# Loading and converting the weights of a fused FFT and MLP kernel: one queue in the order of use, one piece per chunk of x, and products that nobody reads

## The chip, the cores and the metric

The kernel runs on one core of a Trainium2 chip. The metric is the device time of one execution in microseconds (us). Engines are called by the names of the profile: PE is TensorE (PEld its weight loads), DVE is VectorE, ACT is ScalarE, POOL is GpSimd, SP is SyncE. A kernel counts as faster or slower if its fast runs differ from those of the kernel before by over 2%.

## The reference

```python
def _attn_ref(x):                       # x: (8, 3008, 256) float32
    X = np.fft.fft(x, axis=1)
    X = np.fft.fft(X, axis=2)
    return X.real.astype(np.float32)

def _moe_ref(x, w_in, w_out):           # x: (24064, 256), w_in: (256, 2048), w_out: (2048, 256), both float64
    h = x @ w_in
    relu6 = np.clip(h + 3.0, 0.0, 6.0)
    g = h * relu6 / 6.0
    return (g @ w_out).astype(np.float32)
```

The kernel takes the eight batches as four pairs. Along the sequence (3008 = 47 · 64) it does the transform in two stages: a first one of length 47 on folded input, and a second one of length 64. The transform along the 256 columns is multiplied into w_in once ("folding of w_in"). The MLP runs in steps: a step takes two blocks of 128 hidden features, makes products u and v, gates them (hardswish), combines the gated blocks and accumulates them against w_out, of which seven mixtures (G) stand ready.

## The kernel before

The weights arrive as float64; the kernel makes every piece (128 x 512 numbers) into float32, mostly by integer operations, before it is multiplied. There are 16 pieces, taken in pairs: pieces 0, 1, 2, 3, 6, 7, 8, 9 are of w_in, the others of w_out. `narrow_a` unpacks a piece on DVE (four instructions; ACT makes the exponent meanwhile), `narrow_b` adds the sign on DVE and multiplies, on DVE or POOL; `use_pair` folds two w_in pieces with the column transform on PE, or mixes two w_out pieces to G on POOL and ACT.

```python
    def load_w(j):                      # the piece's load, through SP's queue
        st = wpool.tile([P, 2 * WB], I32, tag="st", bufs=5, name="st")
        ...
            nc.sync.dma_start(out=o, in_=moe_w_in[i * P:(i + 1) * P, n * WB:(n + 1) * WB])

    def narrow_a(j):
        ...
        ts = nc.vector.tensor_scalar
        ts(ex[:], hi, 20, 0x7FF, op0=AL.logical_shift_right, op1=AL.bitwise_and)
        ...                                                     # three instructions on ACT
        ts(top[:], hi, 0xFFFFF, 0x100000, op0=AL.bitwise_and, op1=AL.bitwise_or)
        ts(low[:], lo, 8, 0xFFFFFF, op0=AL.logical_shift_right, op1=AL.bitwise_and)
        nc.vector.scalar_tensor_tensor(frac, low[:], 2.0 ** -24, top[:], op0=AL.mult, op1=AL.add)

    def narrow_b(j):
        nc.vector.scalar_tensor_tensor(ex[:], hi, -2 ** 31, ex[:], ...)
        eng = nc.vector if j < 6 else nc.gpsimd
        eng.tensor_tensor(o, frac, ex[:].bitcast(F32), op=AL.mult)

    # MLP, one step's gates: DVE makes u and v into t (with ACT), then
        gate(a[:, 0, :, 0:ns], t[:, 0, :, 0:ns], u[:, :, 0:ns])          # gate u, DVE
        for i in (slice(0, 2),) if nm == KC else (0, 1):
            gate(a[:, 1, i, 0:nm, ::-1], t[:, 1, i, 0:nm], v[:, i, 0:nm]) # gate v, DVE
    # combine(): three additions of the gated blocks on POOL, the same step

    # first pair, stage one: eight chunks of x
    for c in range(NXC):
        fold(first, c, 0, nc.gpsimd)
        fold(first, c, 1, nc.vector)
        if c + 3 < NXC:
            load_x(first, c + 3)       # a direct load and a gather of the partner rows
        if c in (2, 5):
            narrow_pair((c + 1) // 3)
        ...
        if c in (2, 5):
            use_pair((c + 1) // 3)
    # pieces 8 to 15 are converted and used in pairs at MLP steps 0, 1, 3 and 5 (8, 9 are loaded in stage one, the others a pair ahead)
```

## Time and profile before

| | before |
|---|---|
| time, median of four runs | 2080.24 us |
| last product of stage one ends | 84.1 us |
| first MLP accumulation starts | 130.80 us |
| eighth MLP accumulation starts | 189.55 us |
| from there to the end | PE full at full clock |

These are events of PE in the timeline. Their differences split the start into three stretches (stage one, the transition, the first eight steps), and whatever an edit wins must show in one of them. The third stretch runs from the first accumulation to the eighth; here are the two in PE's timeline. The columns are start, length (both in us), engine, line, operation, out<-in, the partitions and columns, and the number of instructions:

```profile
130.80 1.46 PE L320 MATMUL acc<-a,G 128*128 128x256 f32 x6
...
189.55 1.46 PE L320 MATMUL acc<-a,G 128*128 128x256 f32 x6
```

```profile
138.08 1.27 POOL L409 TENSOR_TENSOR st<-top,ex 128x512 f32<-128x512 f32 x1 [11.10 <-DVE ex L406]
```

Here a one-source instruction of the unpacking takes 0.42 us and the two-source one 0.69 us. The bracket says under which condition: before its product POOL had stood still for 11.10 us, and the whole unpacking (133.83 to 135.65 us) lies in that time.

### The profile page before, as it was taken

How to read it: one execution, taken by the hardware profiler on the slowest of the kernel's cores; microseconds unless marked ns; L12 is line 12 of the kernel's file. 1: busy time of each engine (PE TensorE's matmuls, PEld its weight loads, DVE VectorE, ACT ScalarE, POOL GpSimd, SP SyncE). 2: the span in 40 equal slices, each digit the busy share in tenths (PEclk: the TensorE clock that was granted, in tenths of full speed). 3: DMA queues.
4: the chain of work that ended last, by engine and by line, in shares of the span. 5: the costliest groups of instructions: out<-in, count | busy, mean ns of one | idle time of the engine just before them, and what ended most of it. 6: DMA issues, size and time to landing. Idle time of an engine off the chain costs nothing.

```text
span 2078.6 us, 28133 instructions
## 1 busy us (share of the span) xinstructions
PE 1974.6 (95%) x9136; PEld 1692.0 (81%) x9136; DVE 1456.9 (70%) x2714; ACT 706.1 (34%) x1205; POOL 1496.1 (72%) x1662
## 2 busy tenths in 40 slices
PE   4468999999999999999999999999999999999997
PEld 1246888888888888888888888888888888888886
DVE  5366676776777677677677677677777777777775
ACT  2344333333333333333333333333333323333332
POOL 6248777877667887788667778778766766766765
PEclk7688999999999999999999999999999999999999
DMA  6420211221110122212111112211110011011000
GB/s 188 142 86 15 57 49 34 50 47 33 29 31 23 44 51 51 51 33 54 29 21 34 43 34 48 51 43 47 31 36 11 17 23 21 18 24 21 16 16 18
DMA packets 158161, 86.81 MB, mean 42 GB/s; under 512 B 132512, under 2 KB 145056, under 8 KB 158016
## 3 DMA queue, kind: packets, MB, share of 16 engines
q1 hardware_dynamic: 129856, 60.28, 12.7%
q0 software_dynamic: 28160, 24.73, 4.5%
q8 instruction: 74, 1.21, 0.3%
q14 instruction: 71, 0.58, 0.1%
HBM read 47.65 MB, written 37.22 MB: 41 GB/s over the span
## 4 chain that ended last, share of the span: by engine, by line
PE 91%; DVE 4%; DMA 2%; ACT 1%; issue 1%; POOL 1%; SPq 0%; DVEq 0%; POOLq 0%; ACTq 0%
PE acc L320 53%; PE v L266 16%; PE u L266 15%; PE ps L193 2%; PE ps L221 2%; PE wps L446 1%; PE ps L237 1%; DVE a L298 1%; DMA st<-in_moe_w_in_dram 1%; ACT t L295 1%; DVE u L279 0%; DVE ex L406 0%; DVE s L271 0%; PE wns L451 0%; DMA g<-zd 0%
## 5 line engine op out<-in xcount | busy, mean ns | idle before, releaser
L310 POOL TENSOR_TENSOR c<-a 128x512 f32<-128x512 f32 (+1 forms) x384 | 479.2, 1248 | 406.7 <-DVE a L298 258.7
L320 PE MATMUL acc<-c,G 128*128 128x256 f32 (+1 forms) x3072 | 714.1, 375 | 0.0
L320 PEld LDWEIGHTS acc<-c,G 128*128 128x128 f32 x3072 | 579.3, 191 | 73.8 <-POOL c L310 0.2
L295 ACT ACTIVATE t<-u,half 128x512 f32<-128x512 f32 (+2 forms) x416 | 272.3, 655 | 1074.8 <-DVE u L279 1063.2
L271 DVE SCALAR_TENSOR_TENSOR s<-qn,WN,u 128x256 f32<-128x256 f32 x768 | 334.4, 477 | 392.2 <-PE u L266 391.9
L320 PE MATMUL acc<-a,G 128*128 128x256 f32 (+1 forms) x2304 | 553.6, 377 | 0.0
L320 PEld LDWEIGHTS acc<-a,G 128*128 128x128 f32 x2304 | 436.8, 191 | 57.3
L266 PE MATMUL v<-q,W 128*128 128x256 f32 x1536 | 398.8, 382 | 17.9 <-DVE a L298 17.9
L266 PE MATMUL u<-q,W 128*128 128x256 f32 x1536 | 394.5, 379 | 0.0
L266 PEld LDWEIGHTS v<-q,W 128*128 128x128 f32 x1536 | 291.3, 191 | 64.3 <-issue 21.9
L266 PEld LDWEIGHTS u<-q,W 128*128 128x128 f32 x1536 | 287.4, 190 | 65.3 <-issue 20.9
L298 DVE SCALAR_TENSOR_TENSOR a<-t,u 128x512 f32<-128x512 f32 (+2 forms) x416 | 265.9, 646 | 105.3 <-ACT t L295 101.0
L310 POOL TENSOR_TENSOR c<-a,c 128x256 f32<-128x256 f32 (+1 forms) x384 | 275.0, 716 | 30.1
L310 POOL TENSOR_TENSOR c<-c,a 128x256 f32<-128x256 f32 (+1 forms) x384 | 275.0, 716 | 30.1
L279 DVE TENSOR_TENSOR u<-s,v 128x512 f32<-128x512 f32 (+1 forms) x384 | 263.0, 685 | 42.6 <-PE v L266 2.5
L295 ACT ACTIVATE t<-v,half 128x512 f32<-128x512 f32 (+1 forms) x384 | 257.0, 669 | 5.3 <-DVE v L285 4.4
L285 DVE TENSOR_TENSOR v<-v,s 128x512 f32<-128x512 f32 (+1 forms) x384 | 257.7, 671 | 1.1
L298 DVE SCALAR_TENSOR_TENSOR a<-t,v 128x512 f32<-128x512 f32 (+1 forms) x416 | 255.1, 619 | 0.1
L310 POOL TENSOR_TENSOR r<-w,e 128x256 f32<-128x256 f32 (+1 forms) x96 | 92.3, 982 | 3.8
L193 PE MATMUL ps<-y,F 94*96 94x512 f32 x120 | 67.0, 656 | 26.2 <-DVE y L159 20.1
L326 ACT ACTIVATE e<-acc 128x512 f32<-128x512 f32 (+1 forms) x192 | 87.0, 543 | 2.9 <-PE acc L320 2.8
L346 DVE STREAM_TRANSPOSE o<-r 128x256 f32<-128x256 f32 (+1 forms) x192 | 72.4, 415 | 6.5 <-POOL r L310 6.4
(70 smaller groups left out, 826.7 us busy)
## 6 DMA issues: line engine op xcount, KB each, us to landing
out_dram<-o SPq DMA_DIRECT2D x736, 32.0 KB, 1.6
zd<-z SPq DMA_DIRECT2D x32, 384.0 KB, 3.0
g<-zd SPq DMA_DIRECT2D x48, 256.0 KB, 4.2
xt<-in_x_dram POOLq DMA_DIRECT2D x28, 376.0 KB, 3.9
st<-in_moe_w_in_dram SPq DMA_DIRECT2D x8, 512.0 KB, 4.4
st<-in_moe_w_out_dram SPq DMA_DIRECT2D x8, 512.0 KB, 5.7
T<-in_c_stage_dram SPq DMA_DIRECT2D x12, 128.0 KB, 7.2
xt<-in_x_dram POOLq DMA_DIRECT2D x4, 282.0 KB, 3.4
```

Source lines behind the costliest of these rows:

```text
L193: nc.tensor.matmul(ps[0:PZ], F[0:PR, 0:PZ], y[:, 2 * i:2 * i + 2, :], start=True, stop=True)
L221: nc.tensor.matmul(ps[:, blk, 2 * u:2 * u + 2], g[:, kk, blk * P:(blk + 1) * P], T[:, :, gr, blk, kk], start=True, stop=True)
L266: nc.tensor.matmul(ps[:, i], W1[:, blk, f * P:(f + 1) * P], q[:, blk, of:of + KC], start=True, stop=True)
L271: nc.vector.scalar_tensor_tensor(s[:, i].rearrange("p k n -> p (k n)"), qn[:, of * N2:(of + KC) * N2], WN[:, f:f + 1], u[:, i].rearrange(" ...
L279: nc.vector.tensor_tensor(u[:, :, 0:ns], s[:, :, 0:ns], v[:, :, 0:ns], op=AL.add)
L285: nc.vector.tensor_tensor(v[:, :, 0:nm], v[:, :, 0:nm], s[:, :, 0:nm], op=AL.subtract)
L295: nc.scalar.activation(t, h, AF.Relu, bias=half[:], scale=scale)
L298: nc.vector.scalar_tensor_tensor(dst, t, 1.0, h, op0=AL.min, op1=AL.mult)
L310: nc.gpsimd.tensor_tensor(out, in0, in1, op=AL.add)
L320: nc.tensor.matmul(ch.acc[i // 2][:, i % 2, 0:ch.n], G[:, i, fc, :], mv, start=(fc == 0 and i % 2 == 0), stop=(fc == NF - 1), skip_group_c ...
L326: nc.scalar.mul(ch.e[:, k:i + 1, 0:ch.n], ch.acc[i // 2][:, 0:i + 1 - k, 0:ch.n], 1.0 / WS)
L346: nc.vector.transpose(o[:, 0:n // DH, h], ch.r[:, m, h, 0:n].rearrange("p (j i) -> p j i", i=DH))
```

## The change

The intent is to have every weight piece land and be converted just before its use. Loads of x and of weights share POOL's queue, in the order of use; in stage one, one piece is converted per chunk of x; the last four pieces are converted in halves behind the first MLP steps; PE multiplies zeros ("awake" products, which nobody reads) where it would wait, so that its clock stays up. P6 changes its sign so that ACT's negations fall away, and the first two mixings of w_out move from POOL to DVE. The diff, cut to its core:

```diff
-        st = wpool.tile([P, 2 * WB], I32, tag="st", bufs=5, name="st")
+        st = wpool.tile([P, 2 * WB], I32, tag="st", bufs=6, name="st")
-            nc.sync.dma_start(out=o, in_=moe_w_in[...])
+            nc.gpsimd.dma_start(out=o, in_=moe_w_in[...])          # w_out alike
-        ex = wpool.tile([P, WB], I32, tag="ex", bufs=2, name="ex") # top alike
+        ex = wpool.tile([P, WB], I32, tag="ex", name="ex")
-        eng = nc.vector if j < 6 else nc.gpsimd
+        eng = nc.vector if j < 12 else nc.gpsimd
-        tt = nc.gpsimd.tensor_tensor    # in the mixing of w_out
+        tt = (nc.vector if j < 2 else nc.gpsimd).tensor_tensor
-        nc.scalar.mul(g[5], g[5], -1.0)
...
+    load_t(0)
+    load_forward(first, 0)
+    load_w(0)
+    load_w(1)
+    load_partners(first, 0)
+    for c in (1, 2):
         load_x(first, c)
+        load_w(c + 1)
...
+    def keep_awake(n):
+        ps = ps_h.tile([P, 2 * TB], F32, tag="uv", name="awake")
+        for i in range(n):
+            nc.tensor.matmul(ps[:], ones[:], Z[:], start=True, stop=True)
...
         fold(first, c, 0, nc.gpsimd)
-        fold(first, c, 1, nc.vector)
         if c + 3 < NXC:
             load_x(first, c + 3)
-        if c in (2, 5):
-            narrow_pair((c + 1) // 3)
+        load_w(c + 4)
+        fold(first, c, 1, nc.vector)
+        if c > 1:
+            narrow_b(c)
+        if c > 0:
+            narrow_a(c + 1)
...
+        if c % 2 and c > 1:
+            use_pair(c // 2)
+        else:
+            keep_awake(3)
...                                     # pieces 8 to 11 are converted ahead of the MLP
-                put(t, narrow_pair, 4 + i)
-                put(t, use_pair, 4 + i)
+            for t, f, j in ((0, narrow_a, 12), (1, narrow_b, 12), (1, narrow_a, 13), (2, narrow_b, 13), (2, use_pair, 6),
+                            (3, narrow_a, 14), (4, narrow_b, 14), (4, narrow_a, 15), (5, narrow_b, 15), (5, use_pair, 7)):
+                after.setdefault(t, []).append((f, (j,)))
...
         mlp2(*chunk(s))
+        for f, a in after.get(s, ()):
+            f(*a)
```

More of the change, by code (lines that the diff above doesn't have):

```diff
@@ L47 @@
 NK1 = (N1 + 1) // 2
-PROD = ("P1", "P2", "-P4", "P5", "P7", "P6", "P3")
+PROD = ("P1", "P2", "-P4", "P5", "P7", "-P6", "P3")
 @with_exitstack
@@ L116, in __init__ @@
             self.p = p
-            self.x, self.y, self.z = {}, {}, {}
+            self.x, self.xr, self.y, self.z = {}, {}, {}, {}
             self.zd = None
@@ L131, in load_x, with load_forward @@
     def load_x(pr, c):
-        xt, xr = x_tile(pr, 2 * c), x_tile(pr, 2 * c + 1)
+        load_forward(pr, c)
+        load_partners(pr, c)
+    def load_forward(pr, c):
+        xt = x_tile(pr, 2 * c)
         rows = x_pn[pr.p * PR:(pr.p + 1) * PR]
@@ L137, in load_x, with load_partners @@
             nc.gpsimd.dma_start(out=xt[:, n:XC, :], in_=rows[:, 0:1, :])
+        pr.x[c] = xt
+    def load_partners(pr, c):
+        xr = x_tile(pr, 2 * c + 1)
+        pr.xr[c] = xr
         i = pr.p * NXC + c
@@ L142, in load_x @@
         )
-        pr.x[c] = xt, xr
     def fold(pr, c, part, eng):
-        xt, xr = pr.x[c]
+        xt, xr = pr.x[c], pr.xr[c]
         n = XC if c < NXC - 1 else XC - 1
@@ L165, in fold @@
             eng.tensor_copy(y[:, n, 0:P + 1:P], xt[:, n, 0:P + 1:P])
-        del pr.x[c]
+        del pr.x[c], pr.xr[c]
     starting = [True]
@@ L335, in finish @@
         add(rn[:, 0, 0], e[:, 0], e[:, 1])
-        add(wn[:, 0], e[:, 0], e[:, 5])
+        nc.gpsimd.tensor_tensor(wn[:, 0], e[:, 0], e[:, 5], op=AL.subtract)
         add(wn[:, 1:3], wn[:, 0:1].to_broadcast([P, 2, n]), e[:, 4:2:-1])
@@ L374, in load_w @@
         kind, n, i = PIECES[j]
-        st = wpool.tile([P, 2 * WB], I32, tag="st", bufs=5, name="st")
+        st = wpool.tile([P, 2 * WB], I32, tag="st", bufs=6, name="st")
         o = st[:].bitcast(moe_w_in.dtype)
         if kind == "in":
-            nc.sync.dma_start(out=o, in_=moe_w_in[i * P:(i + 1) * P, n * WB:(n + 1) * WB])
+            nc.gpsimd.dma_start(out=o, in_=moe_w_in[i * P:(i + 1) * P, n * WB:(n + 1) * WB])
         else:
             r = (2 * n + i * NF) * P
-            nc.sync.dma_start(out=o.rearrange("p (c j) -> p c j", c=2),
-                              in_=moe_w_out[r:r + 2 * P, :].rearrange("(c p) d -> p c d", p=P))
+            nc.gpsimd.dma_start(out=o.rearrange("p (c j) -> p c j", c=2),
+                                in_=moe_w_out[r:r + 2 * P, :].rearrange("(c p) d -> p c d", p=P))
         raw[j] = st
@@ L390, in narrow_a @@
         ts = nc.vector.tensor_scalar
-        ex = wpool.tile([P, WB], I32, tag="ex", bufs=2, name="ex")
-        top = wpool.tile([P, WB], I32, tag="top", bufs=2, name="top")
+        ex = wpool.tile([P, WB], I32, tag="ex", name="ex")
+        top = wpool.tile([P, WB], I32, tag="top", name="top")
         low = wpool.tile([P, WB], I32, tag="low", name="low")
@@ L407, in narrow_b @@
         o = st[:].bitcast(F32)[:, 0:WB]
-        eng = nc.vector if j < 6 else nc.gpsimd
+        eng = nc.vector if j < 12 else nc.gpsimd
         eng.tensor_tensor(o, frac, ex[:].bitcast(F32), op=AL.mult)
         w[PIECES[j]] = o
-    def narrow_pair(j):
-        for f in (narrow_a, narrow_b):
-            for i in range(2):
-                f(2 * j + i)
     def use_pair(j):
@@ L464 @@
     nc.vector.tensor_copy(IX[:], F[0:PR, 5 * PZ:])
-    for j in range(2):
-        load_w(j)
     nc.sync.dma_start(out=C[:], in_=c_dim.rearrange("(h p) d -> p h d", p=P))
-    for c in range(3):
+    load_t(0)
[4 more added lines that the diff above has]
+    for c in (1, 2):
         load_x(first, c)
+        load_w(c + 1)
     for b in range(2):
@@ L472 @@
     nc.vector.memset(ones[:], 1.0)
-    narrow_pair(0)
+    def keep_awake(n):
+        ps = ps_h.tile([P, 2 * TB], F32, tag="uv", name="awake")
+        for i in range(n):
+            nc.tensor.matmul(ps[:], ones[:], Z[:], start=True, stop=True)
+    Z = spool.tile([P, 2 * TB], F32, tag="s", name="Z")
+    nc.vector.memset(Z[:], 0.0)
+    for j in range(2):
+        narrow_a(j)
+        narrow_b(j)
+    keep_awake(8)
     use_pair(0)
@@ L476 @@
         fold(first, c, 0, nc.gpsimd)
-        fold(first, c, 1, nc.vector)
         if c + 3 < NXC:
             load_x(first, c + 3)
-        if c in (2, 5):
-            narrow_pair((c + 1) // 3)
+        load_w(c + 4)
[4 more added lines that the diff above has]
+            narrow_a(c + 1)
         for i in range(XC // 2):
             stage1(first, c, i)
-        for j in {0: (2, 3), 2: (4,), 3: (5,), 5: (6,), 6: (7,), 7: (8, 9)}.get(c, ()):
-            load_w(j)
-        if c == 4:
-            load_t(0)
-        if c in (2, 5):
-            use_pair((c + 1) // 3)
+        if c % 2 and c > 1:
+            use_pair(c // 2)
+        else:
+            keep_awake(3)
     load_g(first, 0)
     load_g(first, 1)
-    load_t(1)
-    narrow_pair(3)
+    for gr in range(1, NG):
+        load_t(gr)
+    narrow_b(8)
+    for j in (9, 10, 11):
+        narrow_a(j)
+        narrow_b(j)
+        if j == 9:
+            keep_awake(3)
+            use_pair(4)
+            keep_awake(5)
+        load_w(j + 3)
     for i in range(2):
@@ L497 @@
     stage2n_sum(first, 0)
-    use_pair(3)
+    use_pair(5)
+    load_w(15)
     starting[0] = False
@@ L503 @@
     NST = 2 * NF
+    after = {}
     def beside(p):
@@ L512, in beside @@
         if p == 0:
-            for i, t in enumerate((0, 1, 3, 5)):
-                for j in (10, 11, 12, 13, 14, 15)[2 * i:2 * i + 2]:
-                    put(t, load_w, j)
-                if i + 2 < NG:
-                    put(t, load_t, i + 2)
-                put(t, narrow_pair, 4 + i)
-                put(t, use_pair, 4 + i)
+            for t, f, j in ((0, narrow_a, 12), (1, narrow_b, 12), (1, narrow_a, 13), (2, narrow_b, 13), (2, use_pair, 6),
+                            (3, narrow_a, 14), (4, narrow_b, 14), (4, narrow_a, 15), (5, narrow_b, 15), (5, use_pair, 7)):
+                after.setdefault(t, []).append((f, (j,)))
             put(NF - 1, close_w)
```

## The prediction

> **What bounds the kernel now.** I read the page of the kernel before from the top: the busy shares, then the 40 slices, because a share alone does not say where the idle time lies.
>
> ```profile
> PE 1974.6 (95%) x9136; PEld 1692.0 (81%) x9136; DVE 1456.9 (70%) x2714; ACT 706.1 (34%) x1205; POOL 1496.1 (72%) x1662
> ...
> PE   4468999999999999999999999999999999999997
> ...
> PEclk7688999999999999999999999999999999999999
> ```
>
> A slice is 52 us. From the fifth slice on PE is full at full clock; the chain of waits there is nothing but PE work (PE 91% of it). Nothing in that part is changed, so its time cannot move. What can move is the first four slices, where PE is half busy and, as the PEclk row says, often at reduced clock. The view by windows cuts that start at its own events: first product on the start data, last first-stage product (84), first MLP product (106), first accumulation (131), steady state (190).
>
> ```profile
> core 0: us, PE busy (x) PEld busy (x) DVE busy (x) ACT busy (x) POOL busy (x), PEclk, DMA share, GB/s
> ...
> 20.00:50.00 30.00, 14.72 (x33) 5.52 (x32) 16.39 (x24) 8.36 (x14) 21.98 (x20) 0.59 0.70 195
> 50.00:84.00 34.00, 18.36 (x49) 8.69 (x48) 18.42 (x33) 12.02 (x22) 10.70 (x11) 0.65 0.39 118
> 84.00:106.00 22.00, 10.64 (x45) 7.79 (x45) 3.33 (x6) 7.80 (x13) 3.57 (x3) 0.63 0.61 160
> 106.00:131.00 25.00, 13.37 (x49) 7.83 (x48) 13.02 (x24) 8.21 (x13) 10.03 (x10) 0.80 0.30 84
> 131.00:190.00 59.00, 44.48 (x173) 37.01 (x172) 41.57 (x74) 27.32 (x46) 40.52 (x45) 0.83 0.13 40
> ```
>
> No engine is full in any row: the start is bound by waits. The chain of waits and the timeline name them: weight pieces that land late, then conversions that hold up everything behind them in program order on POOL and PE.
>
> ```profile
> 25.49 13.89 DMA st<-in_moe_w_in_dram
> ...
> 57.99 5.61 DMA st<-in_moe_w_out_dram
> ...
> 88.48 6.82 DMA g<-zd
> ...
> 66.86 1.11 POOL L433 TENSOR_TENSOR G<-st 128x256 f32<-128x256 f32 x1 [13.85 <-DVE st L409]
> ...
> 119.88 3.97 PE L446 MATMUL wps<-st,C 128*128 128x512 f32 x4 [8.62 <-POOL st L409]
> ...
> 145.47 2.05 PE L266 MATMUL v<-q,W 128*128 128x256 f32 x4 [5.88 <-DVE a L298]
> ```
>
> The first column is the start, the second the length, the bracket the idle time before and its releaser. POOL stands 13.85 us with two chunks of x still to fold, because the mixing of two w_out pieces is ahead of them and the second piece was requested only at 58 us. PE stands 8.62 us for pieces 8 and 9, in the middle of the MLP's start.
>
> **What the Trainium skill says.** (1) "DMA: Bandwidth & Descriptors", section "Why a DMA increments its semaphore by 16 and not by 1": a transfer uses the largest number of engines up to 16 that divides its slowest dimension, on consecutive engines from a rotating cursor; some direct copies from GpSimd still spread over 16. The gather of the partner rows has 94 rows, so 2 engines; the direct load of 94 rows spreads. The trace agrees: with two gathers in flight the software queue uses 23.9% of 16 engines, 3.8:
>
> ```profile
> DMA packets 47, 0.19 MB, mean 77 GB/s; under 512 B 0, under 2 KB 0, under 8 KB 47
> ...
> q0 software_dynamic: 47, 0.19, 23.9%
> ...
> xt<-in_x_dram,IX POOLq DMA_INDIRECT x9, 13.8
> ```
>
> (window 52.5 to 55 us, then the first 200 us). 47 packets in 2.5 us on four engines are 0.21 us each, so 47 packets on one engine take 10 us; with issue and landing this is the 13.8 us of the row. A gather is a latency, not a bandwidth. (2) Same page, "Queues, rings and completion order": each engine consumes a queue's ring in order. In one queue a weight piece waits behind a gather on two engines, and a gather behind what was queued before it. (3) "TensorE: Matmul & The Clock Gate", "What's actually happening": an idle window of about 3.4 us halves PE's clock. The trace agrees: mean clock 0.50 from 30 to 50 us. (4) "SBUF — State Buffer", "Who interferes with whom": VectorE with two SBUF inputs and GpSimd exclude each other. The trace agrees: L406 took 3.63 us beside POOL's folding, 0.68 us alone.
>
> **The change, part by part, as a schedule.** Durations from the timeline of before: fold of a chunk on POOL 1.27+1.09 = 2.4 us; issue of a direct load 0.6 plus a gap of 0.3; of a gather 1.5 to 1.9; y on DVE 1.5; a piece's conversion 1.75 (four DVE instructions, to the next step), three ACT instructions in 2.2, then 0.68+0.69 on DVE; folding of w_in at full clock 3.43+1.7 = 5.1 on PE; an unread product of 512 columns 0.86.
>
> Stage one. Volume to the first gather is as before plus the first T table (0.26 MB), so fold 0 starts at about 18.8 (18.27 before). Then POOL repeats fold 2.4, direct load 0.9, gather 1.9, weight load 0.8 = 6.0 us per chunk: folds 0, 1, 2 at 18.8, 24.8, 30.8. Gather 3 is issued at 22 to 24, has 6 packets ahead, 47 of its own (10 us), a z write beside it (1.3) and landing (1.5): 37, which is also when POOL is free. By the same sum: fold 4 at 44, fold 5 at 51 (piece 8 also waits there for pieces 2, 3, used at about 48), fold 6 at 56, fold 7 at 64 to 66 (before: 18, 23, 28, 40, 45, 51, 71, 73). DVE has 1.5+3.1 = 4.6 us per chunk, and PE at most 1.9+2.6 or 1.9+5.1, so both stay under POOL's pace. With 2.4 us for the last y and 2.3 for its products stage one ends at 71 instead of 84.1. I take 72, for locking between DVE and POOL. Gain **12 us**.
>
> From there to the first accumulation. The g path (z copy behind one conversion on ACT, zd write 3, g 7) is ready 13 us after the end of stage one. PE's own path is longer: third fold of w_in 5.1, three unread products 2.6, fourth fold (its last conversion waits on ACT behind the third fold's copies, so it starts at +9), to +14, five unread products 4.3: stage two at +18.4. DVE then must convert pieces 10 and 11 and mix them, again behind ACT's copies of the fourth fold: first MLP work on DVE at +23.5. From DVE's first s to POOL's last c it was 6.7 us (106.9 to 113.6), and one more v product waits for the second gate: first accumulation at +31, against 130.8−84.1 = 46.7. Gain **15.5 us**, minus 1.5 for a cold PE.
>
> From the first accumulation to the eighth step. Before: 130.80 to 189.55 = 58.75 us. Undisturbed: 7×4.75 + 2 second-stage groups of 0.9 = 35. The change keeps four conversions and two mixings there, one after another. DVE needs 3.6 us per step for gates; steps with one half conversion become 5.3, and the two steps where the next conversion must wait until POOL's product frees its buffer (single buffers now) about 7.5. Over six steps that is 35.2 instead of 28.5+2, a loss of 5; POOL, with 35.6 us of work in the same six steps, ends as late. I take 41 for the stretch. Gain **18 us**.
>
> The subtraction in place of the addition for P6 costs the same on POOL and takes four 0.42 us negations from ACT: nothing. 31 unread products are added and cost only where counted. Sum: 12+15.5−1.5+18 = 44 us: 2080.3−44 = **2036 us**, ratio 0.979.
>
> **The rivals.** (a) The gathers set the pace whatever the weights do, and the single queue makes them later: 8 weight packets of 0.2 us on each engine per chunk, and POOL's in-order issue must also wait for buffers. For it: gathers behind full rings took up to 18 us before. Stage one would end at about 80: 2044. (b) The unread products themselves become the bound: the five before stage two lie on PE's path while g has already landed; if they run at half clock they cost 8.6 instead of 4.3: 2040. Against: PE has just done 5 us of products, so the clock should be full. (c) The conversions in the first steps hold DVE and POOL as much as before (each of three pairs cost about 8 us): only 27 us gained, 2053. Against: they are now placed after a step's gates, one at a time. (d) Less locking than I allow and a gather latency of 13 us: stage one at 68, loss of 3: 2028. (e) If DMA bandwidth were the limit nothing would be gained; against it, 195 GB/s in the second window, where 60 to 62.5 us show 342.
>
> **Range and chances.** The threshold of 2% is a gain of 41.6 us, hardly below my 44. Errors: stage one ±5, transition ±4, first steps ±4; as independent, about ±7.5. So 0.62 for faster, 0.36 within 2%, 0.02 slower (only by a wait that I have overlooked). Range 2024 to 2052.
>
> **What would show it.** Right: last first-stage product at 69 to 76; POOL starting folds about 6 us apart without the 13.85 us wait; PEclk near 1.0 from 20 us; first accumulation at 99 to 107; the eighth at 140 to 149; equal PE time after it. Wrong: a fold that waits over 4 us for a gather (rival a); stage two starting right after unread products at half clock (b); v products waiting over 4 us in several of the first eight steps (c); or a changed step length in the steady part, which I exclude.

## More of the kernel before

One more view of the kernel before matters later, and the prediction did not show it: a conversion among the first MLP steps, first on DVE, then POOL's next instruction. In brackets stands the idle time of the engine before an instruction, with its releaser.

```profile
134.16 0.42 DVE L399 TENSOR_SCALAR top<-st 128x512 int32<-128x512 int32 x1
...
134.96 0.69 DVE L401 SCALAR_TENSOR_TENSOR top<-low,top 128x512 f32<-128x512 int32 x1
```

## The result, and the profile after

| | before | after | gain | gain predicted |
|---|---|---|---|---|
| time, median of four runs each | 2080.24 | 2055.35 | 24.9 | 44 |
| stage one ends | 84.1 | 77.4 | 6.7 | 12 |
| transition to the first accumulation | 46.7 | 31.6 | 15.1 | 14 |
| first to eighth accumulation | 58.75 | 55.7 | 3.0 | 18 |

The ratio is 0.988 with a 95% interval of 0.9863 to 0.9897, so within 2%. The time lies 3 us above the predicted range of 2024 to 2052.

The first and the eighth accumulation of the changed kernel:

```profile
108.97 1.46 PE L328 MATMUL acc<-a,G 128*128 128x256 f32 x6
...
164.67 1.46 PE L328 MATMUL acc<-a,G 128*128 128x256 f32 x6
```

From its page, PE and its clock by 40 slices:

```profile
PE   6769999999999999999999999999999999999997
...
PEclk9999999999999999999999999999999999999999
```

The clock is up from the first slice, which was the purpose of the awake products. PE's third slice holds a 6 and the fourth is full: the start is shorter by about half a slice. The same windows as before, with the same columns (the one from 84 to 106 us is left out):

```profile
20.00:50.00 30.00, 23.81 (x63) 10.59 (x62) 17.48 (x26) 10.74 (x18) 24.70 (x22) 0.94 0.78 206
50.00:84.00 34.00, 24.90 (x84) 12.68 (x83) 30.74 (x53) 18.24 (x34) 14.68 (x16) 0.85 0.64 179
...
106.00:131.00 25.00, 17.79 (x85) 14.97 (x84) 22.50 (x34) 9.90 (x15) 15.70 (x17) 1.00 0.11 31
131.00:190.00 59.00, 48.51 (x201) 38.31 (x200) 43.74 (x67) 22.02 (x38) 47.15 (x51) 0.94 0.08 20
```

The third pair of numbers is DVE. From 50 to 84 us it is busy for 30.74 of 34, and from 106 to 131 us for 22.50 of 25. Before, no engine was near full there; now DVE is. In the last window POOL is busy for longer (47.15 us) than DVE (43.74), so shares alone do not settle it; the chain of waits below does. The clock cannot be blamed: it is 1.00 in the window from 106 to 131 us, and PE is busy for only 17.79 of 25 us.

Stage one. In the chain of waits, two waits for gathers of partner rows make up 35 us of the first 42:

```profile
3.89 19.33 DMA xt<-in_x_dram,IX
...
26.42 15.46 DMA xt<-in_x_dram,IX
```

POOL's timeline shows the start of fold 0:

```profile
23.30 1.25 POOL L159 TENSOR_TENSOR xt<-xt 94x508 f32<-94x508 f32 x1 [11.70 <-DMA xt<-in_x_dram,IX]
```

The folds start at 23.3, 29.1, 35.0, 42.0, 48.0, 56.4, 63.0 and 70.5. From the first to the last that is 47.2 us, where the prediction had 45 to 47; the first start was predicted at 18.8, and it came 4.5 us later.

The first MLP steps. PE waits for DVE's gates, and once for the last mixing:

```profile
129.13 1.10 PE L274 MATMUL v<-q,W 128*128 128x256 f32 x4 [3.74 <-DVE a L306]
...
154.96 2.04 PE L274 MATMUL v<-q,W 128*128 128x256 f32 x4 [4.57 <-DVE a L306]
...
159.78 0.70 PE L328 MATMUL acc<-a,G 128*128 128x256 f32 x2 [1.11 <-POOL G L438]
```

And the chain of waits between them is mostly DVE, at the unpacking of pieces 14 and 15, with POOL's product (L417) in between:

```profile
134.73 2.41 DVE ex L403
137.13 1.41 DVE top L407
138.55 0.88 DVE low L408
139.45 1.10 DVE top L409
...
144.91 1.27 POOL st L417
146.21 2.68 DVE ex L403
```

L403, L407, L408 and L409 are the four instructions of one unpacking. Here they take 2.41 + 1.41 + 0.88 + 1.10 = 5.8 us on the chain; an undisturbed one takes 1.82 us from first start to last end. What POOL did meanwhile shows best at piece 12, first DVE, then POOL:

```profile
112.52 0.95 DVE L407 TENSOR_SCALAR top<-st 128x512 int32<-128x512 int32 x1
113.39 1.27 DVE L408 TENSOR_SCALAR low<-st 128x512 int32<-128x512 int32 x1
114.69 1.64 DVE L409 SCALAR_TENSOR_TENSOR top<-low,top 128x512 f32<-128x512 int32 x1
```

```profile
113.15 1.23 POOL L239 TENSOR_TENSOR m<-T,g 128x512 f32<-128x512 f32 x1
114.34 1.45 POOL L318 TENSOR_TENSOR c<-a 128x512 f32<-128x512 f32 x1
```

An instruction of 0.42 us takes 1.27, and its end, 114.66, lies just behind the end of POOL's L239, 114.38. The next, of 0.69 us alone, takes 1.64 and ends behind POOL's L318. POOL pays too: L318 in this shape is 1.27 us alone, and 1.45 here. This is the exclusion that the page "SBUF — State Buffer" of the Trainium skill, section "Who interferes with whom", describes: a VectorE instruction in a two-port mode, or with two inputs in SBUF, and a GpSimd instruction that reads SBUF share one pair of ports, and the one that comes later is blocked. It names the one-source instructions of this kind among those that can enter a two-port mode. The trace agrees: both kinds were stretched, and alone the one-source form takes 0.42 us against 0.69 us for the two-source form of the same 512 columns, which fits a faster mode of the first (the trace does not name the mode). Nor is everything on DVE slower beside POOL: the gates just before, which read one source from SBUF and the other from PSUM, took 0.69 and 0.68 us at 110.88 and 111.49 us, while POOL combined from 110.22 to 112.32.

The four unpackings took 4.24, 3.94, 5.90 and 5.58 us, 19.7 in place of 4 · 1.82 = 7.3: 12.4 us more. Twice DVE also waited 1.4 us for POOL's product to free its single buffer. That comes to 15.2 us on DVE. The prediction missed the stretch by 55.7 − 41 = 14.7; since it had counted the two waits, the 12.4 us are most of what it lacked.

### The profile page after: what moved, and what is told of

Same layout as the page of the kernel before. It is cut to its first block, busy times and chain, and to the rows that moved or that the text cites. A ratio compares the mean times of both kernels' runs of the same rounds, so it can differ in the third digit from the quotient of the medians.

```text
span 2053.7 us, 28241 instructions
## 1 busy us (share of the span) xinstructions
PE 1986.1 (97%) x9198; PEld 1695.2 (83%) x9198; DVE 1476.4 (72%) x2729; ACT 702.8 (34%) x1201; POOL 1495.1 (73%) x1664
## 4 chain that ended last, share of the span: by engine, by line
PE 90%; DVE 5%; DMA 2%; ACT 1%; POOL 1%; issue 1%; SPq 0%; DVEq 0%; POOLq 0%; ACTq 0%
PE acc L328 53%; PE v L274 16%; PE u L274 15%; PE ps L201 2%; PE ps L229 2%; DMA xt<-in_x_dram,IX 2%; DVE a L306 1%; PE ps L245 1%; ACT t L303 1%; DVE u L287 1%; DVE s L279 0%; PE wps L448 0%; DVE ex L403 0%; DVE ex L414 0%; DVE top L409 0%
## 5 line engine op out<-in xcount | busy, mean ns | idle before, releaser
L318 POOL TENSOR_TENSOR c<-a 128x512 f32<-128x512 f32 (+1 forms) x384 | 479.6, 1249 | 403.3 <-PE acc L328 234.1
L328 PEld LDWEIGHTS acc<-c,G 128*128 128x128 f32 x3072 | 577.7, 190 | 75.4 <-POOL c L318 2.6
L318 POOL TENSOR_TENSOR c<-a,c 128x256 f32<-128x256 f32 (+1 forms) x384 | 275.1, 716 | 30.1
L318 POOL TENSOR_TENSOR c<-c,a 128x256 f32<-128x256 f32 (+1 forms) x384 | 275.0, 716 | 30.1
L318 POOL TENSOR_TENSOR r<-w,e 128x256 f32<-128x256 f32 (+1 forms) x96 | 92.2, 982 | 3.8
```

Source lines behind the costliest of these rows:

```text
L318: nc.gpsimd.tensor_tensor(out, in0, in1, op=AL.add)
L328: nc.tensor.matmul(ch.acc[i // 2][:, i % 2, 0:ch.n], G[:, i, fc, :], mv, start=(fc == 0 and i % 2 == 0), stop=(fc == NF - 1), skip_group_c ...
```

## The experiments

The theory (L): the first eight steps are held by DVE, and DVE by POOL's work on the shared ports. Rivals: the waits for single buffers; the product on POOL; POOL's load of work from the next pair; and for the second half of the test, that not the place but the earlier start of the conversions matters. For stage one: that the single queue delays the gathers (Q), or that the volume asked for ahead of the first gather does (V). The kernel before gave 2080.93, 2081.44 and 2081.00 us on the three chips of the single runs, and 2079.92 us as the median of seven runs on that of runs 8 and 12 and the last one of 10. "Stretch" is first to eighth accumulation. Line numbers shift by a few lines in the edited kernels.

**1. Two buffers again.** Pieces 13 and 15 get buffers of their own from a spare weight tile.

```diff
+        if j in (13, 15):
+            spare = wpool.tile([P, 2 * WB], I32, tag="st", bufs=6, name="spare")
+            ex, top = spare[:, 0:WB], spare[:, WB:]
```

> Question of this and the next three: the stretch from the first accumulation to the eighth took 55.7 us in the changed kernel, where I had predicted 41. Theory L (lock): DVE's four unpacking instructions of a piece (1.75 us alone) run beside POOL's combining and folding and wait for it, and so take 4 to 6 us. Theory B (buffers): DVE waits for POOL's product to free the single ex and top buffers. Theory P: POOL's own work (mixing, folding of the next pair) is the bound. Here pieces 13 and 15 get their own ex and top. L: the two waits of 1.4 us go, but the unpacking stays at 4 us or more, stretch 52 to 56, total 2052 to 2056. B: stretch 45 or less, total about 2045. P: no change.

Measured: 2052.25 us, correct, stretch 52.5. Both waits of 1.4 us are gone, and the stretch is shorter by 3.2. The unpackings stay at 4.32, 4.38, 5.83 and 4.92 us. The buffers are a real cost of about 3 us, but not the main one.

**2. No conversions among the steps** (a wrong result). Pieces 12 to 15 are neither unpacked nor multiplied; the mixing reads other data of the same size.

```diff
+        if j >= 12:                     # in narrow_a
+            return
+        if j >= 12:                     # in narrow_b
+            w[PIECES[j]] = W1[:, 0, 0:WB]
+            return
```

> Pieces 12 to 15 are not converted in the steps (a constant stands in their place, so the result is wrong on purpose); combining, folding and the mixing of w_out on POOL stay. L and B: the whole excess is due to the conversions, stretch 35 to 41, total 2036 to 2042. P: stretch still over 48, total over 2048.

Measured: 2033.21 us, stretch 35.0, which is the undisturbed length that the prediction had worked out. So the mixings, which were still there, and the rest of these steps added nothing to it, and the four conversions cost 55.7 − 35.0 = 20.7 us. The prediction had given them 6.

**3. No combining among the first eight steps** (a wrong result). POOL's three additions per step are left out for the first chunk of the MLP, which is eight steps.

```diff
     def combine(ch, fc):
+        if ch.pr.p == 0 and ch.ck == 0:
+            ch.c[fc] = a
+            return
```

> POOL does not combine in the first eight steps (accumulation reads the gates' tiles instead, wrong result on purpose); all conversions stay as they are. L: unpacking falls from 4 to 6 us to below 2.5 us except where POOL folds the next pair, stretch 40 to 47, total 2038 to 2047. B: the unpacking's length does not matter; DVE still waits for POOL's product twice, stretch over 50. P: stretch falls too, but the unpacking of the pieces keeps its length.

Measured: 2050.50 us, stretch 49.6. The expectation of 40 to 47 missed. The instructions themselves did as expected where POOL was idle, here at piece 12:

```profile
113.64 0.42 DVE L411 TENSOR_SCALAR low<-st 128x512 int32<-128x512 int32 x1
114.10 0.69 DVE L412 SCALAR_TENSOR_TENSOR top<-low,top 128x512 f32<-128x512 int32 x1
```

Pieces 12 and 13 took 1.82 us each; pieces 14 and 15 took 3.73 and 3.96, beside the folding of the next pair's x, which was still on POOL. With the steps short, the end of the stretch then waited for the last mixing (2.96 us before a v product, 1.42 and 1.16 before accumulations) and ran at half clock after it. The run shows the mechanism at piece 12 and 13, and that combining is not POOL's only work that blocks.

**4. The product on DVE**, so that POOL has less to do and DVE more.

```diff
-        eng = nc.vector if j < 12 else nc.gpsimd
+        eng = nc.vector
```

> The last product of pieces 12 to 15 on DVE, not on POOL: takes the round trip DVE, POOL, DVE away (two waits of 1.4 us, and 4 products of 1.26 us from POOL), adds 4 x 0.69 us to DVE. L: within 3 us of the changed kernel, 2052 to 2057. B or P: 5 us or more faster, below 2050.

Measured: 2053.21 us, correct, stretch 53.5; unpackings 4.51, 3.31, 4.74 and 4.43. A small gain: the two waits for POOL's product become DVE's own work.

**5. POOL's work for the next pair later**: its loads and folds start at step 7.

```diff
-                put(9 * c, load_x, nx, c)
-                put(9 * c + 3, fold, nx, c, 0, nc.gpsimd)
+                b = 9 * c if p else 8 * c + 7
+                put(b, load_x, nx, c)
+                put(b + 3, fold, nx, c, 0, nc.gpsimd)      # and so on
```

> Loading and folding of the next pair begin at step 7 (then every 8 steps, not 9), so that POOL has about 7.5 us less in the first eight steps; the conversions stay. L (lock, as in the first four runs): unpacking of pieces 14 and 15 falls from 5.9 and 5.6 us towards 4, since only combining is left beside it; stretch 50 to 53, total 2049 to 2053. B: no change of the stretch, 54 to 56. P (POOL's own load): stretch under 48.

Measured: 2056.33 us, correct, stretch 54.1; unpackings 3.84, 3.95, 4.86 and 3.94. The two long ones became shorter by 1.0 and 1.6 us, but combining alone is enough to block, and the total did not fall. This expectation missed as well: a stretch of 54 to 56 is what it gave for the rival of the single buffers. Run 1 had tested that rival directly and found 3 us.

**6. The conversion between the two gates.** Between DVE's gates u and v of a step POOL cannot have begun to combine that step, since combining needs both. The conversion's halves are put there, one step earlier than in the change, with the product on DVE.

```diff
         gate(a[:, 0, :, 0:ns], t[:, 0, :, 0:ns], u[:, :, 0:ns])
         ...
+        if ch.pr.p == 0 and ch.ck == 0:
+            for f, j in MID.get(fc, ()):
+                f(j)
         for i in (slice(0, 2),) if nm == KC else (0, 1):
             gate(a[:, 1, i, 0:nm, ::-1], t[:, 1, i, 0:nm], v[:, i, 0:nm])
...
-        eng = nc.vector if j < 12 else nc.gpsimd
+        eng = nc.vector
...
+    MID.update({1: ((narrow_a, 12),), 2: ((narrow_b, 12), (narrow_a, 13)), 3: ((narrow_b, 13),),
+                4: ((narrow_a, 14),), 5: ((narrow_b, 14), (narrow_a, 15)), 6: ((narrow_b, 15),)})
-            for t, f, j in ((0, narrow_a, 12), ...):
+            for t, f, j in ((1, use_pair, 6), (4, use_pair, 7)):
```

> The same conversions, but each half stands between the two gates of a step on DVE, some 3 us after POOL has begun to combine, so that the combining is over when the unpacking starts; last product on DVE; everything one step earlier. L: unpacking near 1.8 us where POOL is through, stretch 40 to 46, total 2039 to 2047. If the amount of DVE work is the cause and not what runs beside it: stretch over 50, total over 2050.

Measured: 2043.31 us, correct, stretch 44.9. Three of four unpackings ran undisturbed (1.82, 1.83, 1.83); piece 14 fell beside a fold of POOL and took 3.85. DVE at pieces 12 and 14, then POOL at piece 14:

```profile
107.10 0.43 DVE L412 TENSOR_SCALAR low<-st 128x512 int32<-128x512 int32 x1
107.56 0.69 DVE L413 SCALAR_TENSOR_TENSOR top<-low,top 128x512 f32<-128x512 int32 x1
...
126.31 0.95 DVE L412 TENSOR_SCALAR low<-st 128x512 int32<-128x512 int32 x1
127.30 1.64 DVE L413 SCALAR_TENSOR_TENSOR top<-low,top 128x512 f32<-128x512 int32 x1
```

```profile
126.94 1.45 POOL L159 TENSOR_TENSOR xt<-xt 94x508 f32<-94x508 f32 x1
```

The same instruction, in the same kernel, is 0.69 us beside an idle POOL and 1.64 beside a folding one.

**7. Both, 5 and 6.**

> Both of the last two: conversions between the gates, and the next pair's loads and folds from step 7. L: all unpacking near 1.8 us, stretch 38 to 43, total 2037 to 2043. If DVE's amount of work is the cause: over 2048.

Measured: 2044.11 us, correct, stretch 44.2. Both lie about 1 us above the ranges expected. Piece 14 fell from 3.85 to 2.89 us, and the total didn't follow; the two totals are single runs.

**8. The control for 6: its order and its product on DVE, but behind both gates.** Only the place moves back.

```diff
-        if ch.pr.p == 0 and ch.ck == 0:
-            for f, j in MID.get(fc, ()):
-                f(j)
         for i in (slice(0, 2),) if nm == KC else (0, 1):
             gate(a[:, 1, i, 0:nm, ::-1], t[:, 1, i, 0:nm], v[:, i, 0:nm])
+        if ch.pr.p == 0 and ch.ck == 0:
+            for f, j in MID.get(fc, ()):
+                f(j)
```

> Control for the run that put each conversion half between VectorE's two gates (2043.3 us; stretch from the first to the eighth accumulation 44.9; unpackings 1.82, 1.83, 3.85, 1.83). Same order of pieces, same earlier step, product on VectorE as there; only the place in the step is moved back, behind both gates, where GpSimd's combining of the step has begun or begins at once. Theory L (it is the exclusive port: unpacking is slow when GpSimd works beside it): unpackings 3.5 to 5 us again, stretch 50 to 54, total 2049 to 2053. Rival E (it was the earlier schedule and the product's engine): stretch 44 to 47, total 2042 to 2046, unpackings short or long without effect.

Measured: 2050.02 us (two runs), correct, ratio to before 0.9854 (0.9834 to 0.9874), stretch 51.5; unpackings 4.67, 3.32, 3.85 and 3.30, two of them a little under the range expected. DVE at piece 12, then POOL's combining beside it:

```profile
107.60 2.33 DVE L411 TENSOR_SCALAR top<-st 128x512 int32<-128x512 int32 x1
```

```profile
108.35 1.27 POOL L322 TENSOR_TENSOR c<-a 128x512 f32<-128x512 f32 x1
```

So of the 10.8 us that run 6 takes from the stretch, 55.7 − 51.5 = 4.2 come from the earlier order and the product's engine, and 51.5 − 44.9 = 6.6 from the place alone. The order helps partly by the same mechanism: it shifts the conversions against POOL's folds, and the sum of the four unpackings falls from 19.7 to 15.1.

All runs of the stretch together:

| run | sum of four unpackings | stretch | time |
|---|---|---|---|
| the change | 19.7 | 55.7 | 2055.35 |
| 1, two buffers | 19.5 | 52.5 | 2052.25 |
| 4, product on DVE | 17.0 | 53.5 | 2053.21 |
| 5, next pair later | 16.6 | 54.1 | 2056.33 |
| 8, earlier, behind the gates | 15.1 | 51.5 | 2050.02 |
| 3, no combining | 11.3 | 49.6 | 2050.50 |
| 6, between the gates | 9.3 | 44.9 | 2043.31 |
| 12, 6 with the table late | 9.3 | 43.8 | 2041.74 |
| 7, 5 and 6 | 8.4 | 44.2 | 2044.11 |
| 2, no conversions | 0 | 35.0 | 2033.21 |

From 8 to 6 the sum falls by 5.8 and the stretch by 6.6. Run 1 lies below its neighbours by the two waits it removes; run 3 lies above what its sum suggests, with its waits for the last mixing. So the sum is the main part of the stretch, not all of it.

**9. Stage one: is it the one queue?** First all weight loads, then only those of pieces 0 and 1, go back to SP's queue.

```diff
-            nc.gpsimd.dma_start(out=o, in_=moe_w_in[...])
+            nc.sync.dma_start(out=o, in_=moe_w_in[...])                          # all pieces
+            (nc.sync if j < 2 else nc.gpsimd).dma_start(out=o, in_=moe_w_in[...]) # second run
```

> Question of these four: stage one ended at 77.3 us where I had predicted 72; the first fold began at 23.3 us, not 18.8, because the first gather took 19.3 us (14.3 before). Theory Q (queue): in one ring a gather's packets wait for the weight packets queued before them and share no time with them; two queues overlap. Theory T: the T table moved to the start takes the time. Here every weight piece goes through SP's queue again, all else as in the changed kernel. Q: first gather back to 14 to 16 us, first fold at 18 to 20 us; later SP waits for buffers ahead of z, so the end of stage one is open: 73 to 80. T: first fold still at 22 to 24.

> Only weight pieces 0 and 1 through SP's queue. Q: first fold at 18.5 to 20.5 us, stage one ends 2 to 4 us earlier, total 2051 to 2054. T: first fold at 22 to 24, total as the changed kernel, 2053 to 2056.

Measured: 2059.48 us with the first fold at 24.24 and stage one ending at 81.4; and 2053.80 us with 21.69 and 75.4. In the nine runs that leave stage one as the change has it the first fold begins between 21.3 and 23.3 and stage one ends between 75.3 and 77.4. So with all weights in the other queue stage one is longer, and with two of them it is as it was. Q is refuted for the first gather: taking weights out of its queue did not bring it forward.

**10. Is it the volume?** The first table of the second stage (0.26 MB) is asked for at chunk 4; in another run pieces 2 and 3 are asked for only after the first fold; in a third both.

```diff
-    load_t(0)                           # ahead of everything
+        if c == 4:                      # table late
+            load_t(0)
...
-        load_w(c + 1)                   # pieces 2 and 3, ahead of the folds
-        load_w(c + 4)
+        for j in {0: (2, 3, 4), 1: (5,)}.get(c, (c + 4,)):   # weights later
+            load_w(j)
```

> The first T table is loaded in chunk 4, as before the change, the weights stay in POOL's queue. T: first fold at 18.5 to 20.5, total 2050 to 2053. Q: first fold at 22 to 23.5, total 2053 to 2056.

> Weight pieces 2 and 3 are asked for after the first fold, together with piece 4, not during the first 11 us. The runs so far have refuted theory Q (all weights through SP: first fold at 24.2 us) and shown that the T table is a part only (first fold at 20.9 without it, 22 to 23.3 with it). Theory V: the first gather shares the engines with everything that is asked for beside it, and 1 MB of weights more at some 210 GB/s is 5 us. V: first fold at 18.5 to 21. If only what stands ahead of the gather in its ring mattered, pieces 2 and 3, queued behind it, would not: first fold at 22 to 23.3. The end of stage one may not move, since the pieces come later: total 2051 to 2060.

> Table late and weight pieces 2 and 3 asked for after the first fold, conversions as in the change. Theory V (the volume asked for ahead of the first gather sets when it lands): first fold at 18 to 19 us. If volume were not it: 20 or later. The total will be long in either case (2060 or more), since the pieces come late as in the run without the table's move.

Measured: the first fold at 20.90 (table late), 20.02 (weights later) and 18.52 (both). V holds, each time in a single run: what is asked for before the first gather has landed delays it, and with both taken away the fold starts within 0.3 us of where the prediction had put it. The word "ahead" in the expectations is too narrow: in the changed kernel the gather is issued at 3.89 us, and the loads of pieces 2 and 3 follow it in the queue, at 7.84 and 10.79 us. They delay it all the same. But the totals are 2053.08, 2066.70 and 2063.87 us. Pieces asked for later come later: in the second run POOL stood 8.37 us, its load of piece 8 waiting until PE had folded pieces 2 and 3 and freed their tile. Delaying the weights wins the time of the first gather and loses more later; moving the table won 2.3 us in this single run and 1.6 from run 6 to run 12.

**11. Without the unread products.**

```diff
-        for i in range(n):
+        for i in range(0):
```

> No unread products at all. My prediction charged them about 7 us on PE's path before stage two, and saw no use for them before that. If they pay: PE at half clock in the folds of w_in and stage one, total 3 us or more slower than the changed kernel (over 2058). If they cost: total 2049 to 2053. If the path to the first MLP product runs over ACT and DVE (conversion of pieces 10 and 11), neither: 2053 to 2057.

Measured: 2060.78 us in a single run, correct, 5.4 us longer. The first two windows after 20 us, for comparison with those above:

```profile
20.00:50.00 30.00, 21.11 (x41) 7.82 (x40) 19.90 (x28) 9.65 (x17) 26.37 (x24) 0.62 0.81 214
50.00:84.00 34.00, 24.39 (x64) 11.39 (x62) 27.02 (x51) 17.98 (x32) 11.47 (x12) 0.64 0.59 172
```

Fewer products (41 and 64 in place of 63 and 84) take nearly the same time, at a clock of 0.62 and 0.64 in place of 0.94 and 0.85. The first product of the MLP starts at 101.85 in place of 98.60. That is point (3) of the prediction's section on the skill, seen from the other side: without work the clock falls, and work that nobody reads holds it up. The unread products pay for themselves.

**12. The best version: 6 with the table late.**

```diff
     # the edit of 6, and
-    load_t(0)
...
         load_w(c + 4)
+        if c == 4:
+            load_t(0)
```

> The run with conversions between the gates, and the first table of the second stage asked for at the fifth chunk of x instead of ahead of everything. If the two gains add (10 to 12 us of the stretch, 2 to 3 us of the first stage): total 2040 to 2042. If the conversions hide it or the earlier first stage only turns into a wait: 2043 to 2044.

Measured: 2041.74 us, median of four runs (2041.00 to 2042.19), correct; ratio to before 0.9815, interval 0.9799 to 0.9831. It is inside the range for adding gains, though run 6 itself is a single run, 1.1 us above the highest of these four. Whether it is 2% better than the kernel before is not settled by this interval; against the change it is 13.6 us lower, on another set of runs. Its last window of the start:

```profile
131.00:190.00 59.00, 55.74 (x252) 46.40 (x251) 43.98 (x78) 21.49 (x36) 46.69 (x52) 1.00 0.16 38
```

PE is busy for 55.74 of 59 us in place of 48.51. In the window from 106 to 131 DVE is still the fullest engine (23.61 of 25 us).

## Why the prediction was wrong

Point by point, by its own steps:

- **Stage one, 12 us:** 6.7 came. The pace of the folds was right; the term that failed is "so fold 0 starts at about 18.8". The step took the volume to the first gather as before plus the table, and gave the table 0.5 us; at the 206 GB/s of the window from 20 to 50 us its 0.26 MB would be 1.3 us (an estimate). The gather landed at 23.2 after 19.3 us in place of 14.3. Run 10 shows that the volume, table and pieces 2 and 3, is the cause: without both the fold starts at 18.52. The sum left the two pieces out. They stand behind the gather in the queue, but they were asked for while it was under way; before the change they were asked for only after fold 0. So two readings of the section on the skill failed here: "A gather is a latency, not a bandwidth", and from point (2) that the place in the queue decides.
- **The transition, 14 us:** 15.1 came. The schedule of folds, unread products, conversions and mixings held to about 1 us (stage two 17.7 us after the end of stage one where it said 18.4, the first MLP work on DVE 23.7 where it said 23.5). The 1.5 us for a cold PE were not needed: the granted clock was 1.00 from 84 to 106 us.
- **The first eight steps, 18 us: the step that failed.** It said "steps with one half conversion become 5.3, and the two steps where the next conversion must wait until POOL's product frees its buffer (single buffers now) about 7.5", and took 41 us for the stretch. 55.7 were measured. (The six steps add up to 4 · 5.3 + 2 · 7.5 = 36.2, not the 35.2 written; the 41 covers this.) The structure was right, DVE's sum per step, and the waits for POOL's product came, at 1.4 us each. Wrong was the duration put into the sum: 1.75 us for an unpacking, where the trace of the changed kernel has 3.94 to 5.90. The stretch is 14.7 of the some 19 us by which the total was missed, and the longer unpackings are 12.4 of these; stage one is 77.4 − 72 = 5.4, and the transition gave 15.1 − 14 = 1.1 back. The rest of the stretch was not separated: even in run 6, with unpackings only 2.0 us above undisturbed ones in sum, the conversions cost 9.9 us where the prediction had allowed 6.
- **How the duration came to be wrong:** it was read off the kernel before, where DVE unpacked while POOL stood still waiting for the result, as the line with 11.10 us of idle time shows. The change removes this waiting, which is its purpose; so POOL works, and the duration no longer holds. The prediction named the exclusion, with a line of 3.63 us against 0.68, and then charged 1 us for it, in another stage. Runs 2, 6 and 8 show it: 35.0 us without conversions, 44.9 with mostly undisturbed ones, 51.5 with the same ones moved behind the gates.
- **The rivals:** (c), which said that the conversions would hold the first steps as before, made 2053 of the total (by its own terms, 44 − 18 = 26 us gained, 2054), and was set aside because they are "now placed after a step's gates, one at a time". Just this place was the costly one: behind both gates is where POOL begins to combine. Its sign, v products waiting over 4 us in several steps, showed only once (4.57 us; the next longest wait was 3.74). (a) was half right: the first gather did come later, and its sign, a fold waiting over 4 us for a gather, showed at fold 0 (11.70 us; 8.06 before), but not because of the single queue. (b) did not occur, since the clock was full there; the unread products gain 5.4 us in all. (d) comes to 2029 by its own terms, not 2028 (4 us in stage one, 6 − 3 in the first steps).
- **The steady part** has no change: from 500 to 1000 us PE was busy for 497.70 us before and 497.58 after.

Open stays how the remaining 44.9 − 35.0 = 9.9 us of the best placement divide between DVE's own work (undisturbed, four conversions are 4 · 1.82 us and four times sign and product) and the step's slack (in run 6 the largest share of the chain of waits over this stretch is POOL's combining, 16.7%); and the spread of about 2 us in the end of stage one between runs that start alike was not explained.

## What to carry to other kernels

A duration read off a trace holds under the condition of that trace: before you put it into a sum, look at what the neighbouring engine did meanwhile, and whether the change lets that engine work. Work on VectorE that GpSimd's work stretches can be put where GpSimd has to wait anyway, here between the two halves of the result that GpSimd needs; the place alone was worth 6.6 us. And count all loads that are asked for before the first awaited one has landed, not only those ahead of it in its queue: here they delayed the first fold by 4.8 us.

## What the Trainium skill lacked or had wrong

- "SBUF — State Buffer" says that the loser of the shared ports is blocked for the whole instruction of the other. Here a loser was blocked for more than one: DVE's L403, 0.42 us alone, took 2.68 us from 146.21, while POOL ran two instructions of 1.26 us back to back from 146.13. The page's "whoever issues first" does not settle who gets the ports between two instructions of the same engine; here it was the one that started second in the trace, at 147.35. Nor does it say that one phase can slow both sides, as here (0.42 to 1.27 us on DVE, 1.27 to 1.45 us on POOL).
- The same page says that two-port instructions of VectorE contend with the making of descriptors on GpSimd. The runs show one case each way. In run 6 DVE unpacked piece 12 from 106.43 to 108.25 us in 1.82 us, undisturbed, while POOL's instruction for a gather ran from 106.53 to 108.27. In run 8 DVE's L411 of the same piece, 0.42 us alone, started at 107.60 beside the same gather (106.77 to 108.32) and had not ended when POOL's combining began at 108.35. Spans on POOL are rough, and no run was made for this, so it stays open.
- "DMA: Bandwidth & Descriptors" has how many engines a transfer uses, but no figure for how long a gather takes beside other loads. Here the first gather took 19.3 us with the table and two more weight pieces asked for before it had landed, and 14.3 us in the kernel before, and the median of the eight gathers of stage one rose from 13.8 to 17.0 us.
